# Spreading streamed weights, moving a score step and the mask builds in a one-core two-layer transformer kernel

## The chip, the cores and the metric

The kernel runs on one core of a Trainium2 chip. The metric is the device time of one execution in microseconds (us). The engines in the profile are PE (TensorE, matmuls), PEld (its weight loads), DVE (VectorE), ACT (ScalarE), POOL (GpSimd) and SP (SyncE, which here issues the weight transfers); a "q" behind a name is the engine's sequencer.

## What is computed

Four layers with residuals: A, B, A, B, on 2048 positions of width 640.

```python
x = x + A(layernorm(x), mem0, Wq, Wk, Wv, Wo, seg_len=32)   # 32 heads of 192
x = x + B(layernorm(x), wqkv, wo)                           # 32 heads of 20
# and both once more with the same weights
# A, for each segment s of 32 positions, one after the other:
h = concatenate([mem, xs], axis=1)          # 8 memory rows + 32 positions = 40
q, k, v = h @ Wq, h @ Wk, h @ Wv
p = softmax(where(mask, q @ k.T * scale, -1e9))
o = (p @ v) @ Wo
mem = o[:, :8]                              # the next segment's memory
# B: each position attends to 8 positions at distances 0, 2, ..., 14
```

A is a recurrence over 64 segments. Its four weight matrices together hold 32 units of 960 KB, and not all of them fit in the on-chip memory.

## The kernel before

**Steps.** Both A layers run at once, the second three segments (LAG) behind the first, as two "lanes" of 40 columns, so that one weight load serves 80 columns (NT). There are 67 steps with A work, then two steps with B work only. In step t A works on a segment of each lane, and B, for the two lanes, on what A gave one and two steps ago (b1 and b2).

**Quads.** A step goes over eight quads of four heads. Quad i has projections of V, K and Q (30 matmuls each, L212, tiles ps_v, ps_k, ps_q), transposes of V (a_vt, L240, ps_vt), the output projection of quad i-2 (a_o, L290, ps_acc), the product of probabilities and V of quad i-1 (a_pv, L266 ps_d and L271 ps_o), some B work, and at the quad's end its own scores (a_s, L254 and L255, ps_s). Around the matmuls ACT copies V (VT, L234) and K (KF, Kz, L222 to L224), and DVE copies Q (QT, L229) and transposed V (Vt, L245). Scores go through Exp on ACT (E, L257) and a mask on DVE (E, L258); a_pv needs that E. A softmax denominator goes through Ln and Exp on ACT (R, L274 and L275) and is multiplied in on DVE (OT, L277 to L279); a_o needs that OT. Behind the last quad stand B's K projection (ps_bk), the layer norm of the next step (ln1: ps_st, ln_m, ln_v, ln_r, then hT), a_pv of quad 7, B's V (ps_bv), a_o of quads 6 and 7, and B's Q (ps_bq).

**Weights.** A unit is the 960 KB of one projection of one quad. Sixteen units (N_RES) stay resident, and sixteen are loaded again in every step into a ring of three tiles (w_ring). Resident are all eight output units and the eight Q units (resident_units takes every third of the V, K, Q units in order). V and K of each quad are streamed. A ring transfer is issued on SP (L194), in program order, once the matmuls that used the same ring tile three units earlier are done.

**Order.** All engines run in the order of the code (a manual schedule over PE, ACT, DVE, POOL and SP). Before the first step build_consts builds constants, among them on POOL the masks of layer B (band, L121 to L146), and issues the loads of B's weights from POOL (L173 to L178). prologue then transposes the first inputs, takes segment 0 (x_take, L481, on POOL), and does the first layer norm.

Of the kernel before, what the change touches and what calls it, by code (L numbers as in the profile page):

```python
# [43 lines left out]
def unit_order():  # L44
    order = []
    for i in range(NQUAD):
        order.append(("v", i))
        order.append(("k", i))
        order.append(("q", i))
        if i >= 2:  # L50
            order.append(("o", i - 2))
    order += [("o", 6), ("o", 7)]
    return order


def resident_units():
    res = {("o", i) for i in range(NQUAD)}
    rest = [u for u in unit_order() if u[0] != "o"]
    n = N_RES - NQUAD
    for j, u in enumerate(rest):  # L60
        if (j * n) // len(rest) != ((j + 1) * n) // len(rest):
            res.add(u)
    return res


class Kernel:
    def __init__(self, ctx, tc, A_x, A_mem0, A_Wq, A_Wk, A_Wv, A_Wo, B_wqkv, B_wo, out):
# [17 lines left out]
        self.units = {}  # L85
        self.resident = resident_units()
        self.xr, self.x1, self.ots, self.qxs = {}, {}, {}, {}
        self.x_load(0, self.nc.sync)
        self.m0 = self.xp.tile([P, D], BF16, name="m0", tag="io2")
        self.nc.vector.memset(self.m0[:], 0.0)  # L90
        self.nc.sync.dma_start(out=self.m0[0:NM, :], in_=self.mem0)
        self.build_consts(B_wqkv, B_wo)

    def build_consts(self, B_wqkv, B_wo):
        nc, cp = self.nc, self.cp
# [21 lines left out]
        self.maskA = mA  # L117

        def band(name, cur):
            m = cp.tile([P, NX], BF16, name=name)  # L120
            nc.gpsimd.memset(m[:], 0.0)  # L121
            for half in range(2):
                off = 0 if half == cur else SEG
                for l in range(2):
                    r0 = 64 * half + SEG * l
                    blk = m[r0:r0 + SEG, SEG * l:SEG * (l + 1)]
                    for w in range(BW):
                        nc.gpsimd.affine_select(out=blk, in_=blk, compare_op=ALU.not_equal, fill=1.0,
                                                base=off - BDIL * w, pattern=[[1, SEG]], channel_multiplier=-1)
            return m  # L130
# [18 lines left out]

        def pers(name, shape, n, dt=BF16, zero=True):  # L150
            ts = []
            for j in range(n):
                t_ = cp.tile(shape, dt, name=f"{name}{j}")
                if zero:
                    nc.vector.memset(t_[:], 0.0)
                ts.append(t_)
            return ts

        self.hT = pers("hT", [P, NC * NT + 88], 2)
        self.KF = pers("KF", [P, 4 * NT + 48], 2)  # L160
        self.Kz = pers("Kz", [P, 4 * NT + 48], 2)
        self.VT = pers("VT", [P, 6 * NT + 48], 1)[0]
        self.Vt = pers("Vt", [P, 1152], 2)
        self.xin = pers("xin", [P, NC, NX], 3)
        self.h2T = pers("h2T", [P, NC, P], 1)[0]
        self.KB = pers("KB", [P, NBC, P], 1)[0]
        self.VB = pers("VB", [P, BH // 2, 2 * BD + 1], 1)[0]
        nc.vector.memset(self.VB[:, :, BD:BD + 1], 1.0)
        self.On = pers("On", [P, 3 * P], 1)[0]
        self.YT = pers("YT", [P, NC, P], 1, zero=False)[0]  # L170
        self.m0T = pers("m0T", [P, NC, NM], 1, zero=False)[0]
        self.wqkv = cp.tile([P, NC, 3 * D], BF16, name="wqkv_sb")
# [7 lines left out]
    def unit(self, kind, i):  # L180
        if (kind, i) in self.units:
            return self.units[(kind, i)]
        nc = self.nc
        res = (kind, i) in self.resident
        if kind == "o":
# [40 lines left out]
    def a_q(self, i, t):  # L226
        ps = self.proj_stationary("q", i, t)
        qt = self.ap2.tile([P, 6, NT], BF16, name="QT")
        self.nc.vector.tensor_copy(out=qt[:], in_=ps[:, 0:6 * NT].rearrange("p (a n) -> p a n", a=6))  # L229
        self.qt = qt  # L230

# [15 lines left out]
    def a_s(self, i):  # L247
        nc = self.nc
        ps = self.one("s")
        sv = ps[:, 0:4 * NT].rearrange("p (h n) -> p h n", h=4)  # L250
        kf, kz, qt = self.KF[i % 2], self.Kz[i % 2], self.qt
        for h in range(4):
# [5 lines left out]
        nc.vector.tensor_tensor(out=e[0:NT], in0=e[0:NT], in1=self.maskA[0:NT, :].unsqueeze(1).to_broadcast([NT, 4, NT]), op=ALU.mult)  # L258
        self.em = e

    def a_pv(self, i):
        nc = self.nc
        em = self.em
        vt = self.Vt[i % 2]
# [213 lines left out]

    def x_take(self, t):
        o = SEG * (t % 4)  # L480
        self.nc.gpsimd.tensor_copy(out=self.xin[t % 3][:, :, 0:SEG], in_=self.xt[:, :, o:o + SEG])  # L481

# [18 lines left out]
    def prologue(self):  # L501
# [7 lines left out]
        self.x_transpose(0)  # L509
        self.x_take(0)  # L510
        self.ln1_sq(0)
# [3 lines left out]
    def step(self, t):  # L515
# [5 lines left out]
        for i in range(NQUAD):  # L521
            if a:
                self.a_v(i, t)
                self.a_k(i, t)
                self.a_vt(i)
                self.a_q(i, t)
                if i >= 2:
                    self.a_o(i - 2)
                if i >= 1:
                    self.a_pv(i - 1)  # L530
# [17 lines left out]
            if i == 3 and b1 is not None:  # L548
                self.b_ln_apply(b1)
            if a:  # L550
                self.a_s(i)
            if i == 2:
# [30 lines left out]
    def run(self, ctx):  # L583
        self.x1p = ctx.enter_context(self.tc.tile_pool(name="x1p", bufs=2))
        self.prologue()
        with self.tc.manual_schedule(engines={ENG.PE, ENG.Activation, ENG.DVE, ENG.Pool, ENG.SP}):
            for t in range(self.n_seg + LAG + 2):
# [57 lines left out]
```

## Time and profile before

| | us |
|---|---|
| median of 6 runs | 4010.48 |
| lowest and highest of them | 4002.35 and 4021.05 |
| the profiled execution, whole | 4016.76 |
| its span (first to last instruction) | 4015.1 |
| PE busy | 3438.8 (86%) |
| DVE busy | 2101.4 (52%) |
| ACT busy | 1804.7 (45%) |
| POOL busy | 58.7 (1%) |
| weight queue q1, share of 16 DMA engines | 79.1% |
| mean granted TensorE clock | 0.992 |

Busy time of PE is modelled and overlaps between neighbouring matmuls. What a stretch costs is read from the start times in the timeline: one projection of 30 matmuls starts 1.07 us before whatever follows it at once.

### The profile page before, as it was taken

What the parts mean: (1) busy time and instruction counts of PE and PEld (TensorE: products, weight loads), DVE (VectorE), ACT (ScalarE), POOL (GpSimd) and SP (SyncE); (2) the same over time, 40 slices, a digit from 0 to 9 for tenths busy, and PEclk for the clock granted to TensorE, in tenths of its full rate; (3) what the DMA queues carried; (4) which work ended last, traced back from release to release, by engine and by line L of the source; (5) the groups of instructions that cost most, each with busy time, mean ns of one, the idle gap of its engine ahead of it and who ended that gap; (6) DMA issues with size and microseconds to landing.
All of it is one profiled execution on the core that took longest, in us unless ns stands there. A gap on an engine that the chain in (4) does not pass through costs nothing.

```text
span 4015.1 us, 187722 instructions
## 1 busy us (share of the span) xinstructions
PE 3438.8 (86%) x86260; PEld 3267.3 (81%) x86260; DVE 2101.4 (52%) x6314; ACT 1804.7 (45%) x4924; POOL 58.7 (1%) x186
## 2 busy tenths in 40 slices
PE   4888888888888888888888888888888888888887
PEld 4788888878888888888888888888888888888886
DVE  2455555555555555555555555555555555555554
ACT  2444444444444444444444444444444444444443
POOL 2000000000000000000000000000000000000000
PEclk9999999999999999999999999999999999999998
DMA  9978878877877887787788778878878878887784
GB/s 323 304 262 285 274 264 270 286 261 267 282 265 268 271 278 269 265 287 268 264 280 275 266 256 295 275 263 283 277 263 267 290 269 276 270 292 257 265 280 149
DMA packets 717752, 1090.16 MB, mean 272 GB/s; under 512 B 18008, under 2 KB 715488, under 8 KB 716960
## 3 DMA queue, kind: packets, MB, share of 16 engines
q1 hardware_dynamic: 714912, 1069.79, 79.1%
q8 instruction: 674, 11.04, 1.1%
q0 software_dynamic: 2048, 8.36, 0.6%
q14 instruction: 118, 0.97, 0.1%
HBM read 1075.46 MB, written 2.62 MB: 269 GB/s over the span
## 4 chain that ended last, share of the span: by engine, by line
PE 58%; DMA 22%; issue 9%; DVE 6%; ACT 4%; POOL 0%; SPq 0%; POOLq 0%; ACTq 0%
DMA w_ring<-in_A_Wk_dram 21%; PE ps_k L212 11%; PE ps_acc L290 11%; PE ps_q L212 11%; PE ps_v L212 11%; PE ps_vt L240 3%; PE ps_o L271 2%; ACT R L275 1%; DVE OT L277 1%; PE ps_s L254 1%; PE ps_bq L362 1%; PE ps_d L266 1%; ACT R L274 1%; PE ps_s L255 1%; PE ps_by L453 1%
## 5 line engine op out<-in xcount | busy, mean ns | idle before, releaser
L212 PEld LDWEIGHTS <-w_ring 128*128 128x128 bf16 x32160 | 1207.6, 100 | 346.0 <-DMA w_ring<-in_A_Wk_dram 222.3
L274 ACT ACTIVATE R<-ps_d 128x320 f32<-128x320 f32 x536 | 233.1, 435 | 928.2 <-PE ps_d L266 924.6
L277 DVE TENSOR_TENSOR OT<-ps_o,R 128x320 bf16<-128x320 f32 x536 | 263.5, 492 | 734.4 <-ACT R L275 730.8
L229 DVE CAST QT<-ps_q 128x480 bf16<-128x480 f32 x536 | 352.2, 657 | 300.8 <-PE ps_q L212 300.3
L212 PE MATMUL ps_k<-hT_308,w_ring 128*128 128x80 bf16 x8160 | 347.1, 203 | 135.8 <-DMA w_ring<-in_A_Wk_dram 97.2
L212 PE MATMUL ps_k<-hT_310,w_ring 128*128 128x80 bf16 x7920 | 334.1, 203 | 129.3 <-DMA w_ring<-in_A_Wk_dram 93.9
L234 ACT CAST VT_320<-ps_v 128x480 bf16<-128x480 f32 x536 | 298.2, 556 | 185.4 <-PE ps_v L212 179.8
L245 DVE COPY Vt_322<-ps_vt 80x384 bf16<-80x384 bf16 x536 | 165.7, 349 | 377.9 <-PE ps_vt L240 376.4
L212 PE MATMUL ps_v<-hT_308,w_ring 128*128 128x80 bf16 x8160 | 341.4, 202 | 18.7 <-issue 12.4
L212 PE MATMUL ps_v<-hT_310,w_ring 128*128 128x80 bf16 x7920 | 330.7, 202 | 18.2 <-issue 16.2
L245 DVE COPY Vt_324<-ps_vt 80x384 bf16<-80x384 bf16 x536 | 165.7, 349 | 293.5 <-PE ps_vt L240 291.1
L240 PE MATMUL ps_vt<-ident,VT_320 128*128 128x128 bf16 x3216 | 273.6, 221 | 22.2 <-issue 18.6
L275 ACT ACTIVATE R<-R 128x320 f32<-128x320 f32 x536 | 251.9, 470 | 16.9
L222 ACT CAST KF_314<-ps_k 128x320 bf16<-128x320 f32 x268 | 113.9, 425 | 295.2 <-PE ps_k L212 295.2
L257 ACT ACTIVATE E<-ps_s 80x320 bf16<-80x320 f32 x536 | 229.9, 429 | 29.2 <-PE ps_s L255 25.7
L222 ACT CAST KF_312<-ps_k 128x320 bf16<-128x320 f32 x268 | 113.9, 425 | 285.0 <-PE ps_k L212 285.0
L240 PEld LDWEIGHTS <-VT_320 128*128 128x128 bf16 x3216 | 194.6, 99 | 25.8 <-issue 21.5
L266 PE MATMUL ps_d<-E,ones 80*128 80x320 bf16 x536 | 162.2, 303 | 50.6 <-DVE E L258 49.6
L258 DVE TENSOR_TENSOR E<-E,maskA 80x320 bf16<-80x320 bf16 x536 | 172.1, 321 | 49.7 <-ACT E L257 43.2
L279 DVE TENSOR_TENSOR OT<-ps_o,R 64x160 bf16<-64x160 f32 x536 | 175.5, 327 | 7.4
L271 PEld LDWEIGHTS <-Vt_324 80*128 80x128 bf16 x2144 | 110.4, 98 | 72.6 <-issue 61.7
L278 DVE TENSOR_TENSOR OT<-ps_o,R 64x160 bf16<-64x160 f32 x536 | 163.8, 306 | 0.0
(623 smaller groups left out, 6299.7 us busy)
## 6 DMA issues: line engine op xcount, KB each, us to landing
w_ring<-in_A_Wv_dram SPq DMA_DIRECT2D x536, 960.0 KB, 7.7
w_ring<-in_A_Wk_dram SPq DMA_DIRECT2D x536, 960.0 KB, 6.0
out_dram<-yout POOLq DMA_DIRECT2D x16, 160.0 KB, 5.3
wqkv_sb<-in_B_wqkv_dram POOLq DMA_DIRECT2D x1, 2400.0 KB, 9.1
xr<-in_A_x_dram POOLq DMA_DIRECT2D x15, 160.0 KB, 5.8
w_q_476<-in_A_Wq_dram SPq DMA_DIRECT2D x1, 960.0 KB, 9.7
w_q_602<-in_A_Wq_dram SPq DMA_DIRECT2D x1, 960.0 KB, 8.6
w_q_746<-in_A_Wq_dram SPq DMA_DIRECT2D x1, 960.0 KB
```

Of the source, the lines that this page charges most:

```text
L212: nc.tensor.matmul(ps[:, NT * n:NT * (n + 1)], lhsT=w[:, c, P * n:P * (n + 1)], rhs=hT[:, NT * c:NT * (c + 1)], start=(c == 0), stop=(c == ...
L222: nc.scalar.copy(out=kf, in_=pv[:, :, 0:3:2, :])
L229: self.nc.vector.tensor_copy(out=qt[:], in_=ps[:, 0:6 * NT].rearrange("p (a n) -> p a n", a=6))
L234: self.nc.scalar.copy(out=self.VT[:, 0:6 * NT], in_=ps[:, 0:6 * NT])
L240: nc.tensor.transpose(out=ps[:, n, :], in_=self.VT[:, NT * n:NT * n + P], identity=self.ident[:])
L245: nc.vector.tensor_copy(out=dst, in_=src[:, pr])
L257: nc.scalar.activation(out=e[0:NT], in_=sv[0:NT], func=ACT.Exp, scale=float(DH) ** -0.5)
L266: nc.tensor.matmul(dn[:, 0:4 * NT], lhsT=self.ones[0:NT, :], rhs=em[0:NT, :, :].rearrange("p h n -> p (h n)"), start=True, stop=True)
L274: nc.scalar.activation(out=rf, in_=dn[:, 0:4 * NT], func=ACT.Ln)
L275: nc.scalar.activation(out=rf, in_=rf, func=ACT.Exp, scale=-1.0)
L277: nc.vector.tensor_tensor(out=ot[:, :, 0:3:2, :], in0=ov[:, :, 0:3:2, :], in1=r[:], op=ALU.mult)
L290: nc.tensor.matmul(self.acc[:, NT * c:NT * (c + 1)], lhsT=w[:, m, P * c:P * (c + 1)], rhs=ot[:, m, :], start=(i == 0 and m == 0 and c == 0 ...
```

## The change

Three things change. The tables that say which sixteen units are streamed are replaced: unit_order now gives each unit a position in the step, from costs written by hand, and streamed_units picks for each of sixteen equally spaced positions the nearest unit not yet picked. The result is, in order of use, v0, q0, k1, v2, o0, v3, o1, k4, o2, k5, o3, q6, v7, q7, o5, o6, where the number is the quad. It was v0, k0, v1, k1 and so on to v7, k7. The ring stays at three tiles and sixteen units stay resident.

The scores of quad i are issued behind V of quad i+1 instead of at the end of quad i; those of quad 7 are issued behind the output projection of quad 5 and ahead of a_pv of quad 6. Q copies and E tiles are kept by quad number for that.

The masks of layer B and the loads of B's weights move from build_consts into build_b_consts, called behind the prologue, and the first x_take runs on DVE instead of POOL.

```diff
 def unit_order():
-    order = []
+    order, at = [], 0
+    def use(kind, i, cost):
+        nonlocal at
+        order.append((at, (kind, i)))
+        at += cost
     for i in range(NQUAD):
...
+        use("v", i, 107)
+        use("k", i, 107 + 34)
+        use("q", i, 107)
         if i >= 2:
...
+            use("o", i - 2, 108)
+        at += 70 + 35
+    at += 280
+    use("o", 6, 108)
+    use("o", 7, 108)
+    return order, at + 90
+
+
+def streamed_units():
+    order, total = unit_order()
+    n = N_UNITS - N_RES
+    res = set()
+    for j in range(n):
+        left = [o for o in order if o[1] not in res]
+        res.add(min(left, key=lambda o: abs(o[0] - j * total / n))[1])
     return res
...
-        self.build_consts(B_wqkv, B_wo)
-
-    def build_consts(self, B_wqkv, B_wo):
+        self.build_consts()
+
+    def build_consts(self):
...
+    def build_b_consts(self, B_wqkv, B_wo):
+        nc, cp = self.nc, self.cp
+        def band(name, cur):
...
-        res = (kind, i) in self.resident
+        res = (kind, i) not in self.streamed
...
-        self.qt = qt
+        self.qts[i] = qt
...
-        kf, kz, qt = self.KF[i % 2], self.Kz[i % 2], self.qt
+        kf, kz, qt = self.KF[i % 2], self.Kz[i % 2], self.qts.pop(i)
...
-        self.em = e
+        self.ems[i] = e
...
-        em = self.em
+        em = self.ems.pop(i)
...
-    def x_take(self, t):
+    def x_take(self, t, eng=None):
...
-        self.x_take(0)
+        self.x_take(0, nc.vector)
...
                 self.a_v(i, t)
+                if i >= 1:
+                    self.a_s(i - 1)
                 self.a_k(i, t)
                 self.a_vt(i)
                 self.a_q(i, t)
                 if i >= 2:
                     self.a_o(i - 2)
+                if i == NQUAD - 1:
+                    self.a_s(i)
                 if i >= 1:
                     self.a_pv(i - 1)
...
-            if a:
-                self.a_s(i)
...
         self.prologue()
+        self.build_b_consts(*self.wB)
```

How the instructions move, first on SP, which issues the weight transfers: the first eight ring transfers of step 1. Before:

```order
L194 DMA w_ring_1837<-in_A_Wv_dram 128x5x768
L194 DMA w_ring_1871<-in_A_Wk_dram 128x5x768
L194 DMA w_ring_1980<-in_A_Wv_dram 128x5x768
L194 DMA w_ring_2014<-in_A_Wk_dram 128x5x768
L194 DMA w_ring_2122<-in_A_Wv_dram 128x5x768
L194 DMA w_ring_2156<-in_A_Wk_dram 128x5x768
L194 DMA w_ring_2295<-in_A_Wv_dram 128x5x768
L194 DMA w_ring_2329<-in_A_Wk_dram 128x5x768
```

The same eight places in the changed kernel:

```order
L205 DMA w_ring_1837<-in_A_Wv_dram 128x5x768
L205 DMA w_ring_1914<-in_A_Wq_dram 128x5x768
L205 DMA w_ring_2012<-in_A_Wk_dram 128x5x768
L205 DMA w_ring_2108<-in_A_Wv_dram 128x5x768
L205 DMA w_ring_2230<-in_A_Wo_dram 128x6x640
L205 DMA w_ring_2281<-in_A_Wv_dram 128x5x768
L205 DMA w_ring_2403<-in_A_Wo_dram 128x6x640
L205 DMA w_ring_2501<-in_A_Wk_dram 128x5x768
```

Neighbours in a ring were V and K of one quad, used one right behind the other; now at most one or two units of a quad are streamed, and eight transfers reach to quad 4 instead of quad 3.

Second, ACT at the start of a step in mid-kernel (VT and KF are the copies of V and K, ln_v and ln_r the layer norm of B, E the Exp of the scores). Before:

```order
L234 CAST VT_320<-ps_v 128x480
L222 CAST KF_312<-ps_k 128x320
L223 CAST Kz_316<-ps_k 64x2x80
L224 CAST Kz_316<-ps_k 64x2x80
L326 ACTIVATE ln_v<-ln_v,eps_t 128x64
L328 ACTIVATE ln_r<-ln_v 128x64
L257 ACTIVATE E<-ps_s 80x320
L234 CAST VT_320<-ps_v 128x480
```

In the changed kernel:

```order
L245 CAST VT_114<-ps_v 128x480
L233 CAST KF_106<-ps_k 128x320
L234 CAST Kz_110<-ps_k 64x2x80
L235 CAST Kz_110<-ps_k 64x2x80
L337 ACTIVATE ln_v<-ln_v,eps_t 128x64
L339 ACTIVATE ln_r<-ln_v 128x64
L245 CAST VT_114<-ps_v 128x480
L268 ACTIVATE E<-ps_s 80x320
```

The Exp of quad 0's scores and the copy of quad 1's V have changed places.

Third, ACT behind the last quad (R is the denominator, KB the copy of B's K, VB of B's V). Before:

```order
L274 ACTIVATE R<-ps_d 128x320
L275 ACTIVATE R<-R 128x320
L257 ACTIVATE E<-ps_s 80x320
L368 CAST KB_334<-ps_bk 128x6x64
L326 ACTIVATE ln_v<-ln_v,eps_t 128x64
L328 ACTIVATE ln_r<-ln_v 128x64
```

In the changed kernel:

```order
L268 ACTIVATE E<-ps_s 80x320
L285 ACTIVATE R<-ps_d 128x320
L286 ACTIVATE R<-R 128x320
L379 CAST KB_128<-ps_bk 128x6x64
L337 ACTIVATE ln_v<-ln_v,eps_t 128x64
L339 ACTIVATE ln_r<-ln_v 128x64
```

The Exp of quad 7's scores stands ahead of the denominator of quad 6 instead of behind it; the layer norm and the denominator of quad 7 follow as before.

## Rows read from the trace of the kernel before

**Rows 1.** The page: busy time with instruction counts, and the chain that ended last.

```profile
PE 3438.8 (86%) x86260; PEld 3267.3 (81%) x86260; DVE 2101.4 (52%) x6314; ACT 1804.7 (45%) x4924; POOL 58.7 (1%) x186
PE 58%; DMA 22%; issue 9%; DVE 6%; ACT 4%; POOL 0%; SPq 0%; POOLq 0%; ACTq 0%
```

**Rows 2.** Timeline of PE: V of quad 0 in steps 1 and 66.

```profile
112.26 0.91 PE L212 MATMUL ps_v<-hT_310,w_ring 128*128 128x80 bf16 x21 [0.33 <-DVE hT_310 L304]
3923.62 0.56 PE L212 MATMUL ps_v<-hT_308,w_ring 128*128 128x80 bf16 x11
```

**Rows 3.** Waits of PE from 520 to 3520 us: total, times, longest.

```profile
PE ps_k L212 <- DMA w_ring<-in_A_Wk_dram: 139.9, 155, 2.1
PE ps_k L212 <- issue: 55.3, 38, 2.4
...
PE ps_bt L441 <- issue: 0.2, 1, 0.2
```

**Rows 4.** Timeline of SP and PE, quads 0 and 1, then 6 and 7: start, us, work, idle before.

```profile
2054.70 0.37 SPq L194 DMA_DIRECT2D w_ring<-in_A_Wk_dram  x1
2055.78 0.37 SPq L194 DMA_DIRECT2D w_ring<-in_A_Wv_dram  x1
...
2055.92 1.24 PE L212 MATMUL ps_q<-hT_308,w_q_476 128*128 128x80 bf16 x30
2056.99 0.31 PE L316 MATMUL ps_st<-x_54939,ones 128*128 128x64 bf16 x5
...
2057.91 0.20 PE L254 MATMUL ps_s<-QT,KF_312 128*128 128x80 bf16 x1 [0.46 <-DVE QT L229]
...
2058.18 1.24 PE L212 MATMUL ps_v<-hT_308,w_ring 128*128 128x80 bf16 x30
2060.12 0.35 PE L212 MATMUL ps_k<-hT_308,w_ring 128*128 128x80 bf16 x5 [0.69 <-DMA w_ring<-in_A_Wk_dram]
...
2035.61 1.24 PE L212 MATMUL ps_q<-hT_310,w_q_1452 128*128 128x80 bf16 x30
2039.19 0.99 PE L212 MATMUL ps_v<-hT_310,w_ring 128*128 128x80 bf16 x23
```

**Rows 5.** The page: weight queue and instruction queue: packets, MB, share of 16 engines.

```profile
q1 hardware_dynamic: 714912, 1069.79, 79.1%
q8 instruction: 674, 11.04, 1.1%
```

**Rows 6.** Timeline of PE: two gaps that nothing released, and their neighbours.

```profile
2087.97 0.84 PE L212 MATMUL ps_q<-hT_308,w_q_1275 128*128 128x80 bf16 x19 [1.62 <-issue]
...
2094.47 0.23 PE L212 MATMUL ps_k<-hT_308,w_ring 128*128 128x80 bf16 x2 [1.56 <-issue]
```

**Rows 7.** Stretches of one step: length, busy time by engine, PEclk, DMA share, GB/s.

```profile
2046.20:2058.20 12.00, 10.60 (x269) 9.88 (x266) 7.18 (x22) 5.04 (x14) 0.00 (x0) 1.00 0.43 146
2070.00:2102.00 32.00, 28.41 (x743) 27.54 (x740) 17.23 (x53) 15.41 (x43) 0.00 (x0) 1.00 0.88 286
```

**Rows 8.** Timeline of PE and DVE behind the last quad.

```profile
2048.30 0.30 PE L266 MATMUL ps_d<-E,ones 80*128 80x320 bf16 x1 [0.78 <-DVE E L258]
2051.66 1.06 PE L290 MATMUL ps_acc<-OT,w_o_1800 128*128 128x80 bf16 x25 [0.16 <-DVE OT L279]
...
2047.93 0.32 DVE L258 TENSOR_TENSOR E<-E,maskA 80x320 bf16<-80x320 bf16 x1
2048.28 0.23 DVE L322 TENSOR_SCALAR ln_m<-ps_st 128x64 f32<-128x64 f32 x1
```

**Rows 9.** Start of the kernel: timelines of POOL and SP, then one stretch.

```profile
25.09 0.32 POOL L481 COPY xin_326<-XT_367 128x160 bf16<-128x160 bf16 x1
3.22 1.03 SPq L194 DMA_DIRECT2D w_ring<-in_A_Wv_dram  x1
30.88 0.37 SPq L194 DMA_DIRECT2D w_ring<-in_A_Wk_dram  x1
...
32.00:112.00 80.00, 48.25 (x1107) 43.86 (x1105) 23.02 (x64) 21.59 (x57) 0.00 (x0) 0.98 1.05 367
```

More of the change, by code (lines that the diff above doesn't have):

```diff
@@ L44, in unit_order @@
 def unit_order():
-    order = []
+    order, at = [], 0
[3 more added lines that the diff above has]
+        at += cost
     for i in range(NQUAD):
-        order.append(("v", i))
-        order.append(("k", i))
-        order.append(("q", i))
+        use("v", i, 107)
+        use("k", i, 107 + 34)
+        use("q", i, 107)
         if i >= 2:
[L51 to L62, printed above, removed]
+            use("o", i - 2, 108)
[11 more added lines that the diff above has]
+        res.add(min(left, key=lambda o: abs(o[0] - j * total / n))[1])
     return res
@@ L85, in __init__ @@
         self.units = {}
-        self.resident = resident_units()
-        self.xr, self.x1, self.ots, self.qxs = {}, {}, {}, {}
+        self.streamed = streamed_units()
+        self.wB = (B_wqkv, B_wo)
+        self.xr, self.x1, self.ots, self.qxs, self.ems, self.qts = {}, {}, {}, {}, {}, {}
         self.x_load(0, self.nc.sync)
@@ L117, in build_consts, with pers @@
         self.maskA = mA
+        def pers(name, shape, n, dt=BF16, zero=True):
+            ts = []
+            for j in range(n):
+                t_ = cp.tile(shape, dt, name=f"{name}{j}")
+                if zero:
+                    nc.vector.memset(t_[:], 0.0)
+                ts.append(t_)
+            return ts
+        self.hT = pers("hT", [P, NC * NT + 88], 2)
+        self.KF = pers("KF", [P, 4 * NT + 48], 2)
+        self.Kz = pers("Kz", [P, 4 * NT + 48], 2)
+        self.VT = pers("VT", [P, 6 * NT + 48], 1)[0]
+        self.Vt = pers("Vt", [P, 1152], 2)
+        self.xin = pers("xin", [P, NC, NX], 3)
+        self.h2T = pers("h2T", [P, NC, P], 1)[0]
+        self.KB = pers("KB", [P, NBC, P], 1)[0]
+        self.VB = pers("VB", [P, BH // 2, 2 * BD + 1], 1)[0]
+        nc.vector.memset(self.VB[:, :, BD:BD + 1], 1.0)
+        self.On = pers("On", [P, 3 * P], 1)[0]
+        self.YT = pers("YT", [P, NC, P], 1, zero=False)[0]
+        self.m0T = pers("m0T", [P, NC, NM], 1, zero=False)[0]
+    def build_b_consts(self, B_wqkv, B_wo):
+        nc, cp = self.nc, self.cp
         def band(name, cur):
@@ L148, in build_consts @@
         self.hmask = hm
[L150 to L171, printed above, removed]
         self.wqkv = cp.tile([P, NC, 3 * D], BF16, name="wqkv_sb")
@@ L477, in x_transpose @@
         self.xt = xt
-    def x_take(self, t):
+    def x_take(self, t, eng=None):
         o = SEG * (t % 4)
-        self.nc.gpsimd.tensor_copy(out=self.xin[t % 3][:, :, 0:SEG], in_=self.xt[:, :, o:o + SEG])
+        (eng or self.nc.gpsimd).tensor_copy(out=self.xin[t % 3][:, :, 0:SEG], in_=self.xt[:, :, o:o + SEG])
     def y_store(self, g):
```

## The prediction

> **What bounds the kernel now.** I read the chain of waits first, then the waits of PE, then the timeline of one step. PE is 86% busy and no other engine over 52%, but the chain lies on PE for only 58% of the span; 22% of it is DMA and 9% "issue", time in which PE waited for nothing that the profile shows [rows 1]. So the place to look is what holds PE up. From V of quad 0 in step 1 to the same in step 66 there are 3923.62 - 112.26 = 3811.36 us, or 58.64 us for each of 65 steps [rows 2]. In the 3000 us from 520 to 3520, that is 51.2 steps, PE idled 139.9 us in 155 gaps for a streamed K, and 169.6 us in 175 gaps of "issue" (ten rows of the view, of which the first and the last are shown) [rows 3]. These idle times are counted from modelled ends and come out short: K started 1.94 us after V at 2058.18, where a projection with nothing to wait for hands on after 1.07 us (Q at 2055.92, the next at 2056.99), which makes 0.87 us lost where the row says 0.69 [rows 4]. I add 0.18 us to each gap. A step then loses (139.9 + 155 x 0.18) / 51.2 = 3.3 us to K and (169.6 + 175 x 0.18) / 51.2 = 3.9 us to "issue".
>
> **Why K is late.** K of quad 1 uses the ring tile that V of quad 0 frees. It was issued at 2054.70 and used at 2060.12, 5.4 us later, with PE waiting; the rate was not short, since just before it, from 2046.2 to 2058.2, the DMA engines were 43% busy [rows 4, 7]. The two ring tiles of a quad fall free 1.08 us apart, so transfers come in pairs (2054.70 and 2055.78) [rows 4].
>
> **What "issue" is.** The instruction queue moved 11.04 MB in 674 packets, 16.4 KB each, and PE has 2 x 86260 instructions [rows 1, 5]: 11.04 MB over 172520 is 64 bytes each, so a packet holds 256 PE instructions, 128 matmuls with their loads, and a step (172520 over 67 steps, 2575 instructions) takes 10.06 packets. Two "issue" gaps stand at 2087.97 and 2094.47, 6.50 us apart [rows 6]; between their ends PE ran the last 19 matmuls of Q, then o3, ps_d, ps_o, ps_bt, ps_s, V, and 28 of K, 128 in all. I read the gaps as PE at the end of one packet with the next not there. They follow the weight transfers: from 2070 to 2102, with the DMA engines 88% busy, this step has them; from 2046.2 to 2058.2, at 43%, PE waits for no "issue" at all [rows 7]. In the stretch between, PE stood for K, and the packets caught up. So the fetch competes with the transfers, and a change in when transfers run moves it too. Take away a gap of 1.56 + 0.18 us and a packet's work lasts 4.76 us.
>
> **The change, part by part.**
>
> *Streamed units.* Same number, sixteen of 960 KB. From 32 to 112 us, with the DMA engines never free, they moved 367 GB/s [rows 9]: 983040 bytes take 2.68 us, sixteen 42.9 us, which fits under any step forecast here. A unit is now issued when the one three places earlier is released, 1.07 us after that one's first matmul. The closest such pair in the new order is q6 and o5: q6 started at 2035.61 and v7 at 2039.19, 3.58 us later, with nothing waited for [rows 4]; v7, k7 and q7 add 3.21 us, and transposes and scores a little. Less 1.07 us for q6 itself, at least 5.7 us are left where 5.4 us are needed. All others have six or seven projections from one first matmul to the other, or B's work behind the last quad besides four. So the K waits go: -3.3 us a step. Bounds: all of it, or half, if transfers that queue behind one another still arrive late.
>
> *Instruction fetch.* Now 3.9 us fall on quads 4 to 8, some 32 us or 6.4 packets: 0.61 us a packet. After the change the transfers run through the whole step, so all ten packets meet them, and none is hidden under a wait for K: at 0.61 us each that is 6.1 us, the upper bound. The lower is nothing, as in the 43% stretch. Against the upper bound speaks that pairs are gone: a fetch then found up to two transfers ahead (5.4 us), and now mostly one at some stage of its 2.68 us. With two the packet period was 6.50 us; less 2.68 us, 3.8 us is below the 4.76 us of a packet's work and would not be felt. I take a little under half of the upper bound, 2.9 us, since transfers 3.3 us apart on average with 2.68 us of data each still overlap at times: -1.0 us a step.
>
> The Trainium skill ("Runtime: NRT & Kernel Launch", section "Instruction fetch mechanics") says that instructions come in 16 KiB blocks fetched ahead, and that crossing a block boundary is mostly hidden. The block size agrees with the 16.4 KB a packet above; that it is hidden does not agree with the two gaps. By that rule the gaps would have another cause and stay as they are, which is the third rival.
>
> *Scores behind the next V.* In quad 0 the scores waited 0.46 us for the copy of Q (DVE), 0.64 with the correction [rows 4]. V of quad 1 now covers that: -0.6 us. If V were late, it would be back. The Exp falls behind the copy of V on ACT; K, the transposes and Q (two projections, over 2.1 us) stand between the scores and ps_d, against 0.32 us for the mask [rows 8] and an Exp of similar length, so nothing waits for it.
>
> *Scores of quad 7.* Behind the last quad ps_d waited 0.78 us for E [rows 8]. The scores now run earlier and that wait goes. But nothing is gained: the end is set by a chain on DVE and ACT. OT of quad 6 was followed by the mask of E at 2047.93 and this by ln_m at 2048.28; the layer norm and the denominator of quad 7 on ACT come next, and o7 on PE waited for their OT, to 2051.66 [rows 8]. Without the mask in this chain ln_m could start 0.35 us earlier; but the scores now stand ahead of ps_d of quad 6 (0.28 us of PE), and its denominator waits for one Exp more on ACT (some 0.2 us). The wait moves from ps_d to o7. I count 0; bounds -0.9 and +0.2 us.
>
> *Masks behind the first inputs.* The first x_take stood on POOL behind the masks until 25.41 us [rows 9]. On DVE it can run as soon as the inputs are transposed, at most 16 us earlier. But step 0 must bring in all 32 units and is bound by transfers (share 1.05 from 32 to 112 us) [rows 9]. Four were issued by 3.22 us, enough until about 13 us; the next at 30.88 us, data from 32. Of those 19 idle us the loads of B's weights (3.28 MB, at 367 GB/s 8.9 us) used about nine, and these will now compete. What is won is 19 - 9 = 10 us, once. Bounds 0 and 16.
>
> **Sum.** -3.3 - 1.0 - 0.6 + 0 = -4.9 us a step, 53.7 us instead of 58.64. For the 66 steps from step 1 that is -323 us, and -10 at the start: 4016.8 - 333 = 3684 us against the profiled execution, which lies 6.3 us above the median; so 3677 us.
>
> **Rivals.**
> 1. *Every packet pays.* The fetch term takes its upper bound, 6.1 us: -3.3 + 2.2 - 0.6 = -1.7 us a step, 4010.5 - 112 - 10 = 3888 us. For it: the share of DMA will be near 80% everywhere. Against: the pairs are gone. Chance 0.08. The Trainium skill ("DMA: Bandwidth & Descriptors", section "Queues, rings and completion order") says that each DMA engine takes turns between queues packet by packet; by it a fetch would not stand behind a whole transfer, and undoing the pairs would help less, which leans to this rival.
> 2. *Half of the K waits stay*, as waits for other units: +1.65 us a step, 3677 + 109 = 3786 us. For it: o5 has only some 0.3 to 0.9 us to spare. Chance 0.12.
> 3. *The "issue" gaps have another cause* and stay at 3.9 us: +1.0 us a step, 3677 + 66 = 3743 us. Chance 0.11.
> 4. *Fetch is no longer felt*: -3.9 us instead of -1.0: -7.8 us a step, 4010.5 - 515 - 10 = 3486 us. Chance 0.08.
> 5. *Slower.* Fetch sets the pace: ten packets a step break even with 58.64 us at 5.83 us a packet (58.64 over 10.06). If spread transfers keep a queue at every moment, and packets take 6.0 us on average, against 6.50 us in the pair of gaps read above, a step takes 60.4 us: 4010.5 + 116 - 10 = 4117 us. Against: that needs two transfers ahead all the time, while sixteen of 2.68 us fill 71% of 60.4 us. Chance 0.03.
>
> The forecast itself has 0.58. A fetch term of 1.0 us gives -6.8 us a step and 3550 us; one of 5.2 us gives -2.6 us and 3829 us, which also takes in rivals 2 and 3. I give 3550 to 3830 us; rivals 1, 4 and 5 (0.19) lie outside. A measurement of this kernel can tell about 0.3% (12 us) from no change. Slower by more has the 0.03 of rival 5, within it 0.02 (the far end of rival 1), faster 0.95.
>
> **What would show it.** Right: no wait for w_ring among the larger waits of PE; "issue" near 2.9 us a step and spread over all quads, the quiet start and end of a step included; the wait of ps_s for QT gone; the wait of ps_d for E replaced by one of ps_acc for OT of nearly the same size; step 1 beginning near 102 us. Wrong: waits of ps_acc or ps_q for w_ring; "issue" well over 3.9 us a step; step 1 beginning at 112 us, or before 97.

## The result and the profile after

The changed kernel takes 3691.4 us (median of 10 runs, 3682.18 to 3708.18), against 4015.36 us of the kernel before (20 runs by then). The ratio is 0.9196, 95% interval 0.918 to 0.9211. Forecast were 3677 us and 3550 to 3830 us. The profiled execution took 3697.04 us, its span is 3695.0 us.

The page after: busy time with instruction counts, queues, and the chain that ended last. They answer to [rows 1, 5].

```profile
PE 3380.5 (91%) x86260; PEld 3247.1 (88%) x86260; DVE 2108.2 (57%) x6315; ACT 1791.1 (48%) x4924; POOL 62.5 (2%) x185
q1 hardware_dynamic: 765600, 1069.79, 87.3%
q8 instruction: 674, 11.04, 1.2%
PE 80%; issue 9%; DVE 5%; DMA 4%; ACT 3%; POOL 0%; POOLq 0%; SPq 0%; ACTq 0%
```

The chain that was on PE for 58% is now on it for 80%, and the share of DMA fell from 22% to 4%. "Issue" kept its 9%. The bytes and the instruction packets are the same.

V of quad 0 in steps 1 and 66, the rows that answer to [rows 2]:

```profile
103.07 1.13 PE L223 MATMUL ps_v<-hT_104,w_ring 128*128 128x80 bf16 x27 [0.33 <-DVE hT_104 L315]
3608.48 0.70 PE L223 MATMUL ps_v<-hT_102,w_ring 128*128 128x80 bf16 x15
```

That is 3505.41 us over 65 steps, 53.93 us a step instead of 58.64: 4.71 us less where 4.9 were forecast. Step 1 begins 9.2 us earlier where 10 were forecast.

Waits of PE from 520 to 3520 us (total, times, longest), against [rows 3]:

```profile
PE ps_o L282 <- DVE OT L290: 39.9, 56, 0.9
PE ps_k L223 <- issue: 38.0, 44, 2.2
PE ps_acc L301 <- issue: 26.0, 30, 1.8
PE ps_v L223 <- issue: 24.4, 35, 2.5
PE ps_q L223 <- issue: 21.1, 31, 1.8
PE ps_acc L301 <- DVE OT L290: 12.3, 55, 0.2
...
PE ps_acc L301 <- DMA w_ring<-in_A_Wo_dram: 1.7, 4, 0.5
```

Waits for w_ring are down to 1.7 us in 55.6 steps, from 139.9 us. The gaps of "issue" sum to 146.7 us in 180 gaps (13 rows of the view), which with 0.18 us more for each, as in the prediction, is 3.2 us a step. No row names QT as what the scores wait for. The masked E no longer holds up ps_d; a wait of ps_o for OT of nearly that size stands in its place.

### The profile page after: what moved, and what is told of

Its sections match the earlier page's. It is cut to its first block, busy times and chain, and to the rows that moved or that the text cites. A ratio compares the mean times of both kernels' runs of the same rounds, so it can differ in the third digit from the quotient of the medians.

```text
span 3695.0 us, 187869 instructions
## 1 busy us (share of the span) xinstructions
PE 3380.5 (91%) x86260; PEld 3247.1 (88%) x86260; DVE 2108.2 (57%) x6315; ACT 1791.1 (48%) x4924; POOL 62.5 (2%) x185
## 3 DMA queue, kind: packets, MB, share of 16 engines
q1 hardware_dynamic: 765600, 1069.79, 87.3%
## 4 chain that ended last, share of the span: by engine, by line
PE 80%; issue 9%; DVE 5%; DMA 4%; ACT 3%; POOL 0%; POOLq 0%; SPq 0%; ACTq 0%
PE ps_v L223 15%; PE ps_k L223 15%; PE ps_q L223 15%; PE ps_acc L301 13%; PE ps_vt L251 5%; PE ps_o L282 3%; DMA w_ring<-in_A_Wo_dram 2%; PE ps_s L265 2%; PE ps_s L266 2%; DVE OT L288 2%; PE ps_d L277 2%; PE ps_bk L373 2%; PE ps_bq L373 2%; PE ps_bs L417 1%; PE ps_by L464 1%
## 5 line engine op out<-in xcount | busy, mean ns | idle before, releaser
L223 PEld LDWEIGHTS <-w_ring 128*128 128x128 bf16 x20100 | 776.7, 100 | 88.9 <-issue 67.8
L288 DVE TENSOR_TENSOR OT<-ps_o,R 128x320 bf16<-128x320 f32 x536 | 263.5, 492 | 662.4 <-ACT R L286 610.9
L301 PE MATMUL ps_acc<-OT,w_ring 128*128 128x80 bf16 x12060 | 508.1, 203 | 35.0 <-issue 23.3
L301 PEld LDWEIGHTS <-w_ring 128*128 128x128 bf16 x12060 | 466.5, 100 | 45.3 <-issue 26.5
L223 PE MATMUL ps_v<-hT_102,w_ring 128*128 128x80 bf16 x4080 | 172.0, 202 | 13.3 <-issue 9.0
L290 DVE TENSOR_TENSOR OT<-ps_o,R 64x160 bf16<-64x160 f32 x536 | 175.5, 327 | 7.4
L282 PE MATMUL ps_o<-E,Vt_118 80*128 80x80 bf16 x2144 | 122.8, 201 | 57.1 <-DVE OT L290 48.5
L223 PE MATMUL ps_v<-hT_104,w_ring 128*128 128x80 bf16 x3960 | 165.7, 202 | 7.7 <-issue 6.9
```

What stands on the lines that cost most here:

```text
L223: nc.tensor.matmul(ps[:, NT * n:NT * (n + 1)], lhsT=w[:, c, P * n:P * (n + 1)], rhs=hT[:, NT * c:NT * (c + 1)], start=(c == 0), stop=(c == ...
L282: nc.tensor.matmul(ov[:, pr, b, :], lhsT=vt[0:NT, 512 * pr + w0:512 * pr + w0 + P], rhs=em[0:NT, 2 * pr + j, :], start=st, stop=sp)
L288: nc.vector.tensor_tensor(out=ot[:, :, 0:3:2, :], in0=ov[:, :, 0:3:2, :], in1=r[:], op=ALU.mult)
L301: nc.tensor.matmul(self.acc[:, NT * c:NT * (c + 1)], lhsT=w[:, m, P * c:P * (c + 1)], rhs=ot[:, m, :], start=(i == 0 and m == 0 and c == 0 ...
```

## The experiments

In what follows the fetch term is always the "issue" rows of PE from 520 to 3320 us with 0.18 us added to each gap, per step; by this stretch it is 4.0 us before and 3.2 us after. The ring term is the same for waits for w_ring. A step is the time from V of quad 0 in step 1 to the same in step 66, over 65, from the one profiled execution of each kernel. Ratios are to the kernel before on the same chip; the chips differ between experiments, so kernels are set against one another by their ratios.

| kernel | V of quad 0, step 1 | step 66 | a step | fetch term | ring term |
|---|---|---|---|---|---|
| before | 112.26 | 3923.62 | 58.64 | 4.0 | 3.3 |
| changed | 103.07 | 3608.48 | 53.93 | 3.2 | 0.0 |
| new units alone | 108.21 | 3631.35 | 54.20 | 2.7 | 0.2 |
| scores alone | 113.36 | 3907.85 | 58.38 | 3.6 | 4.0 |
| masks alone | 105.07 | 3935.97 | 58.94 | 4.1 | 3.2 |
| changed, no transfers | 102.83 | 3368.55 | 50.24 | 0 | 0 |
| before, no transfers | 113.77 | 3438.14 | 51.14 | 0 | 0 |
| changed, smaller transfers | 103.61 | 3376.53 | 50.35 | 0.1 | 0 |
| paced halves | 123.88 | 3611.11 | 53.65 | 2.3 | 0.6 |
| unpaced halves | 117.12 | 3620.77 | 53.90 | 3.3 | 0.0 |
| own tile for quad 7 | 102.87 | 3598.94 | 53.79 | 3.2 | 0.1 |
| quad 7 early | 103.78 | 3584.65 | 53.55 | 3.2 | 0.1 |
| paced halves, quad 7 early | 123.94 | 3592.64 | 53.37 | 2.6 | 0.6 |
| layer norm cut in two | 103.01 | 3581.86 | 53.52 | 3.8 | 0.2 |

### The parts alone

Only the new choice of streamed units, in the kernel before:

```diff
-        self.resident = resident_units()
+        self.streamed = streamed_units()
...
-        res = (kind, i) in self.resident
+        res = (kind, i) not in self.streamed
```

> The new choice of streamed units alone; scores and mask builds stay as in the kernel before. Theory (the K waits and part of the issue gaps go, the 0.6 us of quad 0 and the start stay): the measured 4.7 us a step less 0.6 us, times 66, is 270 us off: 3745 us, ratio 0.933, with the wait of ps_s for QT still there. Rival (the fetch of instructions sets the pace, so whatever PE saves elsewhere is given back): the scores' part is worth nothing and this alone gives all but the start, 3700 us, ratio 0.922.

Measured: 3721.65 us, ratio 0.9237 (0.9218 to 0.9256). The rival's 0.922 lies inside the interval, the first reading's 0.933 far outside. A step took 54.20 us, 4.4 us less than before. The wait for QT is there as before:

```profile
PE ps_s L261 <- DVE QT L236: 24.2, 53, 0.5
```

The fetch term was 2.7 us, lower than in the whole change. This part makes most of the gain, and what the other two add on top is less than it would be alone.

Only the scores behind the next V:

```diff
                 self.a_v(i, t)
+                if i >= 1:
+                    self.a_s(i - 1)
...
+                if i == NQUAD - 1:
+                    self.a_s(i)
...
-            if a:
-                self.a_s(i)
```

> The scores behind the next V alone; streamed units and masks as before. Two readings. Sum of parts: 0.6 us a step as predicted for quad 0, 66 times 0.6 is 40 us off: 3975 us, ratio 0.990. Rival, which I hold likelier: with the old units K of quad 1 lands 5.4 us after its issue whatever PE does meanwhile, so the 0.6 us turn into a longer wait of ps_k for w_ring (3.3 to some 3.9 us a step) and the time stays within 10 us of before, ratio 0.998 to 1.001.

Measured: 3994.16 us, ratio 0.9911 (0.9886 to 0.9936). The number is that of the sum of parts, 0.990, and not that of the rival that I held likelier, 0.998 or more. But the rival's mechanism is in the trace, and at its full size: waits of ps_k for w_ring rose from 139.9 to 158.7 us in 3000 us, and V waits for w_ring too.

```profile
PE ps_k L217 <- DMA w_ring<-in_A_Wk_dram: 158.7, 142, 3.1
...
PE ps_v L217 <- DMA w_ring<-in_A_Wv_dram: 16.3, 31, 0.7
```

That is 3.3 before and 4.0 us a step now, so the ring took the 0.6 us of quad 0 back. The time fell all the same, since the fetch term fell from 4.0 to 3.6 us (it is 4.1 in the masks alone, on the same chip), which neither reading had. Why it fell was not tested. That the sum of parts gave the right number here is luck.

Only the masks and the first x_take:

```diff
-        self.x_take(0)
+        self.x_take(0, nc.vector)
...
         self.prologue()
+        self.build_b_consts(*self.wB)
```

> The mask builds behind the first inputs and the first x_take on DVE alone. Theory (step 0 is bound by its 32 units and the loads of layer B's weights): V of quad 0 starts at about 12.4 us as in the changed kernel, but with the old units the ring is full after four transfers instead of six, all the same transfers go on early; step 1 begins 9 to 10 us earlier, ratio 0.9977. Rival (all the 16 us by which PE starts earlier count): ratio 0.996. Rival (B's weights now compete and take it all back): ratio 1.000.

Measured: 4020.41 us, ratio 0.9986 (0.9966 to 1.0005), which by itself can't be told from no change; it rules out the second reading, 0.996, and neither of the others. Its trace is clearer:

```profile
12.38 2.16 PE L216 MATMUL ps_v<-hT,w_ring 128*128 128x80 bf16 x30 [2.48 <-DVE hT L341]
...
105.07 1.09 PE L216 MATMUL ps_v<-hT,w_ring 128*128 128x80 bf16 x26 [0.33 <-DVE hT L308]
```

V of quad 0 started at 12.38 us instead of 28.70, and step 1 at 105.07 instead of 112.26, 7.2 us earlier where 9 to 10 were expected. So 9 of the 16 us were given back in step 0: the first reading's mechanism, with a size that was too large. The new units alone brought step 1 forward by 4.1 us (108.21). There SP issues six weight transfers before it first has to wait for a ring tile, instead of four, which I take to be the reason; together the two make 9.2 us, not 11.

The product of the three ratios is 0.9142, the whole change 0.9196: the parts overlap by some 0.5%, which the widths of the four intervals make uncertain by about 0.4%.

### What "issue" is

The transfers taken away. In the changed kernel and in the kernel before, the ring is three fixed tiles, loaded in step 0 only; from step 1 on the projections use whatever unit lies there, so the results differ and the work is the same.

```diff
-            t_ = self.wring.tile([P, 3840], BF16, name="w_ring")
+            t_ = self.ring[self.nring % RING]
+            self.nring += 1
...
-        nc.sync.dma_start(out=v, in_=src)
+        if res or self.nring <= 16:
+            nc.sync.dma_start(out=v, in_=src)
```

> The changed kernel without its transfers from step 1 on: the three ring tiles keep what step 0 loaded, so projections use wrong weights and only the work is the same. Theory (the issue gaps are PE waiting for its instructions behind weight transfers): with no transfers they are gone, 3.2 us of the 53.96 us of a step; the step takes 50.2 to 50.9 us, the kernel 3465 to 3500 us. Rival (the gaps have another cause, in PE's own issue): they stay at about 3 us a step, and only the few waits for w_ring go: 3680 to 3695 us.

> The kernel before without its transfers from step 1 on (the three ring tiles keep what step 0 loaded; wrong weights, same work). Theory: the K waits (3.3 us a step) and the issue gaps (3.9 us) both go, a step takes 51.0 to 51.6 us, 0.6 us more than the changed kernel without transfers, because the scores of quad 0 still wait for QT: 3510 to 3550 us. Rival (gaps of another cause): only the K waits go, some 55 us a step, 3780 us.

Measured: 3454.42 us, a little under the range expected, and 3524.61 us, inside it; steps of 50.24 and 51.14 us. All waits of PE from 520 to 3320 us, first of the changed kernel without transfers, then of the kernel before without them:

```profile
PE ps_o L286 <- DVE OT L294: 40.0, 56, 0.9
PE ps_acc L305 <- DVE OT L294: 12.6, 56, 0.2
```

```profile
PE ps_d L270 <- DVE E L262: 42.6, 54, 0.8
PE ps_s L258 <- DVE QT L233: 25.2, 55, 0.5
PE ps_acc L294 <- DVE OT L283: 9.0, 55, 0.2
```

There is no "issue" row left in 2800 us. PE runs the same instructions, fetched in 674 packets as before; so the gaps are made by the weight transfers. That they are waits for instructions shows in where they stand. Counted along the whole stretch from 520 to 3320 us, matmuls, weight loads and PE's semaphore instructions together, all 163 gaps of the kernel before stand at the same place in a block of 256 instructions, and so do all 168 of the changed kernel; the prediction had read it from two. The transfers cost the changed kernel 53.93 - 50.24 = 3.69 us a step. The two lists show the scores' move bare: the wait for QT gone, the wait for E turned into one for OT, a step 0.9 us shorter (0.6 were expected).

Then smaller transfers at the same packet size: 3 of 5 or 3 of 6 row blocks of each unit from step 1 on. The other row blocks are left out, so the results differ; PE's work is the same.

```diff
-        nc.sync.dma_start(out=v, in_=src)
+        n = v.shape[1] if res or self.nring <= 16 else 3
+        nc.sync.dma_start(out=v[:, 0:n, :], in_=src[:, 0:n, :])
```

> The changed kernel with smaller transfers from step 1 on: of each streamed unit only three of five (V, K, Q) or three of six (output) row blocks are loaded, 56% of the bytes with packets of the same size; wrong weights, same work. Theory (what counts is how much is queued ahead of a fetch; a packet stalls when more than about 1.9 us of transfers are ahead): with at most 1.6 us in one transfer the gaps nearly go, 0.3 to 0.9 us a step instead of 3.2, 3485 to 3530 us. Rival (what counts is whether a transfer is in flight at all): the gaps shrink with the busy share, to some 1.8 us a step, 3590 us.

Measured: 3467.4 us, 50.35 us a step, better than the theory expected. The stretch from 520 to 3320 us (length, busy by engine, PEclk, DMA share, GB/s), of this kernel and then of the changed kernel:

```profile
520.00:3320.00 2800.00, 2743.68 (x71568) 2664.94 (x71564) 1734.41 (x5221) 1478.79 (x4083) 36.10 (x81) 1.00 0.61 181
```

```profile
520.00:3320.00 2800.00, 2601.58 (x66813) 2504.45 (x66810) 1629.60 (x4881) 1385.20 (x3812) 34.89 (x78) 1.00 0.90 296
```

And its "issue" rows, all of them:

```profile
PE ps_q L227 <- issue: 2.5, 4, 0.9
PE ps_acc L305 <- issue: 1.4, 4, 0.5
PE ps_by L468 <- issue: 0.5, 1, 0.5
```

The DMA engines are busy 61% of the time instead of 90%, two thirds, and the gaps fall to 0.1 us a step, a thirtieth. So the gaps don't follow the busy share in proportion. This run alone can't separate share from depth, since both fell.

Depth can be worked out from the issues and packets in the traces. At the moment PE enters a block of 256 instructions, count the bytes of the weight transfers whose issue has begun, less those that have landed, at 367 GB/s, and see whether PE has a gap at the end of that block. There are 480 blocks before and 522 after, from 520 to 3320 us.

| queued, us | under 0.3 | 0.3 to 1.1 | 1.1 to 1.9 | 1.9 to 2.7 | 2.7 to 3.5 | 3.5 to 4.3 | over 4.3 |
|---|---|---|---|---|---|---|---|
| blocks with a gap, before | 0% | 0% | 0% | 20% | 46% | 55% | 47% |
| blocks with a gap, after | 0% | 0% | 0% | 19% | 56% | 62% | 31% |

Up to 4.3 us the two kernels lie close together. The count is rough at its deep end, because a transfer that was issued a moment ago is in it and need not be ahead of the fetch: with nothing queued, its first packet starts 1.0 us after the issue. On average 2.9 us were queued before and 2.7 us after: the pairs are gone, but the times when nothing was queued are gone too (lowest tenth 0 before, 1.0 us after). What did get rarer is a deep queue, over 3.5 us: 40% of the blocks before, 21% after.

The start of the fetch itself says it more sharply. The instruction packet that belongs to the next block starts 0.2 us (median) after PE enters a block when there are no transfers. Where it started within 2.25 us of that, PE had no gap: 0 of 180 blocks before, 0 of 247 after. Where it started more than 3.5 us later, PE had one in 94 of 119 blocks before and in 54 of 59 after. At a gap, PE went on 2.5 us (median) after the packet's start in both kernels. In the kernel with smaller transfers 1.3 us were queued on average, and no block saw 3.5 us or more.

The Trainium skill ("DMA: Bandwidth & Descriptors", section "Queues, rings and completion order") has a DMA engine take turns between queues packet by packet. By that rule the depth of the weight queue would not matter to a fetch. The two counts above say that it does here.

### Can the queue be kept short at the same bytes?

Each ring transfer from step 1 on issued in two parts; the second part waits on SP for an 8-byte transfer that reads the next copy on ACT or DVE. One kernel with that pacing, one that issues the second part at once.

```diff
+        self.nc.sync.dma_start(out=v[:, 0:3, :], in_=src[:, 0:3, :])
...
+        self.nc.sync.dma_start(out=s[0:1, 0:4], in_=ap)
+        self.nc.sync.dma_start(out=v[:, 3:, :], in_=src[:, 3:, :])
```

> The changed kernel with the same bytes, but each ring transfer of step 1 on in two parts (3 of 5 or 3 of 6 row blocks, then the rest); the second part is held back on SP by an 8-byte transfer that waits for the next copy on ACT or DVE, 1 to 2.5 us later (not for o5, which has no time to spare). Theory (a fetch pays for what is queued ahead of it): the queue ahead falls from mostly 2 to 4 us to mostly under 2, the issue gaps from 3.4 to 1.0 to 2.0 us a step, 3590 to 3640 us, ratio 0.895 to 0.907, at the same share of DMA. Rival (bytes or busy share count, not depth): gaps stay, 3691 us or more, since the later landing brings waits for w_ring.

> As the paced version, but the second part follows the first at once: twice the transfers, no spacing. Theory (depth of the queue): nothing gained, 3685 to 3720 us, ratio 0.918 to 0.926. Rival (smaller single transfers are what helps, by turns between queues): as the paced version, 3590 to 3640 us.

Measured: 3709.75 us, ratio 0.9217 (0.9195 to 0.9239) paced, and 3713.96 us, 0.9229 (0.9206 to 0.9251) unpaced. Neither is better than the changed kernel. The unpaced time is as expected. The paced time is that of the rival, 3691 us or more, and so are its waits for w_ring. Part of the time was lost at the start: in step 0 SP stood in waits with resident units queued behind them, and step 1 began at 123.88 and 117.12 us. In the steps after, the theory holds in its direction but not in its size. The fetch term is 2.3 us paced (1.0 to 2.0 were expected) against 3.3 unpaced, and a step 53.65 against 53.90 us: about half of the saving came back as waits for parts that landed late. These are the rows of the paced kernel from 520 to 3320 us:

```profile
PE ps_k L260 <- DMA w_ring<-in_A_Wk_dram: 12.6, 20, 1.6
...
PE ps_acc L343 <- DMA w_ring<-in_A_Wo_dram: 5.0, 11, 1.2
...
PE ps_v L260 <- DMA w_ring<-in_A_Wv_dram: 4.4, 7, 1.0
```

The pacing also hardly shortened the queue. Counted as in the table above, 2.6 us were queued on average in the paced kernel, and 2.7 us in the unpaced and in the changed one; over 3.5 us were queued at 13% of the blocks instead of 21%. So the queue that the theory spoke of, mostly under 2 us at the same bytes, was not reached, and what it would give stays open. A deeper ring was not tried; a fourth tile could be had by keeping one unit less resident. The unpaced kernel does show that more and smaller transfers at the same queue change nothing.

### The chain behind the last quad

First the suspect that the waits name, the single ps_o tile: quad 7 gets a tile of its own in PSUM, the memory that matmuls write to.

```diff
-        ops = self.one("o")
+        ops = self.one("o") if i < NQUAD - 1 else self.big("ps_o7")
```

> The changed kernel with the product of quad 7 in a PSUM tile of its own (one of the four big tiles) instead of the single ps_o. Theory (behind the last quad a chain on DVE and ACT sets the end: OT of quad 6, layer norm, denominator and OT of quad 7): the wait of ps_o for OT, some 0.9 us a step, moves to ps_acc of quad 7, which waits for its OT; within 0.3% of 3691 us, ratio to before 0.917 to 0.922. Rival (the single ps_o is the cause): 0.8 us a step off, 53 us, ratio 0.906.

Measured: 3689.63 us, ratio 0.9151 (0.9119 to 0.9183); in the trace 53.79 us a step. The wait of ps_o for OT is gone and one of ps_acc for OT L288 has come:

```profile
PE ps_acc L301 <- DVE OT L288: 35.7, 47, 0.8
```

The wait moved, as the chain says; the step is 0.14 us shorter. The ratio is a little under the 0.917 to 0.922 expected. Its interval overlaps that of the changed kernel (0.918 to 0.9211), so a small gain is left open.

Then the chain itself: quad 7's product ahead of the layer norm on all engines.

```diff
-        if nt < T:
-            self.ln1(nt)
-            self.ln1_apply(nt)
         if a:
             self.a_pv(7)
+        if nt < T:
+            self.ln1(nt)
+            self.ln1_apply(nt)
```

> The changed kernel with the product of quad 7 ahead of the next step's layer norm, on all engines, and in a PSUM tile of its own. Theory (behind the last quad the chain OT of quad 6, layer norm, denominator of quad 7, OT of quad 7 sets the end): taking the layer norm out of it frees some 1.0 us a step, 3620 to 3640 us, ratio 0.902 to 0.907. Rival: the layer norm then ends late and V of the next step's quad 0 waits for hT as long: 3685 to 3695 us.

Measured: 3674.32 us, ratio 0.9131 (0.9108 to 0.9153), a step 53.55 us: less than expected, more than nothing. The waits for OT are gone; V of the next step waits for hT instead:

```profile
PE ps_v L223 <- DVE hT L315: 30.3, 48, 0.8
```

With the paced halves on top:

> Paced halves and the early product of quad 7 together. If both theories hold and their gains add, 3520 to 3575 us, ratio 0.877 to 0.891. Rival (a shorter step loads the queue more and the fetch takes back half of it, as between the scores alone and the whole change): 3570 to 3610 us.

Measured: 3687.25 us, 0.9173 (0.9146 to 0.92), slower than both expectations. A step took 53.37 us, and step 1 came late as in the paced kernel (123.94 us). Against the 53.55 us of the early product alone, the pacing again gives only 0.2 us a step.

Last, the layer norm cut in two around OT of quad 7:

```diff
+            m, v = self.ln_moments(ps)
+            xc = self.ln_center(x0, m)
         if a:
             self.a_pv(7)
+        if nt < T:
+            r = self.ln_rstd(v)
+            self.ln_scale(xc, r, self.lanes(self.hT[nt % 2][:, 0:NC * NT])[:, :, :, NM:LT])
```

> The changed kernel with quad 7's product in a PSUM tile of its own, and the next layer norm cut in two: its work on DVE up to the centred input ahead of OT of quad 7, its Ln, Exp and scaling behind. Theory (the chain behind the last quad sets the end; in the early version the whole layer norm on DVE stood between OT of quad 7 and hT, and V waited 0.6 us for hT): both waits go, a step is 52.7 to 53.2 us against 53.55 in the early version, 3625 to 3655 us, ratio 0.903 to 0.910. Rival (the fetch of instructions takes back what the tail gives): a step stays at 53.4 to 53.6 us, 3665 to 3680 us, with more issue gaps.

Measured: 3663.59 us, ratio 0.9105 (0.9081 to 0.913), the best kernel of this study, 1.0% below the changed kernel. A step took 53.52 us in the profiled execution. Its first waits of PE from 520 to 3320 us:

```profile
PE ps_k L223 <- issue: 48.0, 51, 2.4
PE ps_acc L301 <- issue: 36.7, 39, 3.0
PE ps_v L223 <- issue: 28.1, 48, 1.3
PE ps_q L223 <- issue: 26.0, 34, 1.6
```

Waits for OT, E and hT are gone, which with 0.18 us for each gap is 1.3 us a step less than in the changed kernel. But the fetch term rose from 3.2 to 3.8 us with 204 gaps instead of 168, waits for w_ring rose by 0.1 us, and the step fell by only 0.4. The median stands 28 us below that of the changed kernel, the same 0.4 us a step. So the theory was right about the waits and the rival about the step: the chain was broken, and the fetch took about half of it back. Some 0.15 us a step is not accounted for.

## Why the prediction was right, point by point

**K waits, forecast -3.3 us a step.** Right: 0.04 us a step is left. The ring gives each unit the 5.4 us it needs, the closest pair q6 and o5 included; that pair gives three of the four waits there are, on ps_acc.

**Instruction fetch, forecast 2.9 us after, -1.0.** Right in the cause, which the kernels without transfers show, and near in size: 3.2 us, -0.8. The reason given was only half right. I argued that pairs are gone and a fetch finds a shorter queue. Measured, the mean queue was nearly the same (2.9 and 2.7 us), and a block about as likely to end in a gap at a given depth. What fell is mostly the length of a gap: by the "issue" rows from 520 to 3320 us there were 3.4 gaps a step of 0.99 us on average before (163 in 47.7 steps) and 3.2 of 0.82 us after (168 in 51.9). The traces show which got rarer: fetches that started more than 3.5 us late, 119 of 480 blocks before (25%) with 126 of the 161.5 us of gaps behind them, and 59 of 522 after (11%) with 71.5 of 138.1 us. The deep queues did go with the pairs, as the reason says; what it left out is that the empty ones went too.

**Where the gaps stand.** I expected them in all quads and in the quiet end of the step too. They came to the start of the step: 47 of the 168 gaps stand in quads 0 to 2, where before there was none. Behind the last quad there is one, where there were nine.

**Scores of quad 0, forecast -0.6.** Right as a mechanism: the wait is gone, and without transfers the whole scores' move is worth 0.9 us a step. With the transfers it is worth less: on top of the new units a step fell from 54.20 to 53.93 us. The ratios agree: 0.9237 to 0.9196 is 16 us, of which step 1 beginning earlier is 5, and the rest some 0.2 us a step. The fetch term rose meanwhile from 2.7 to 3.2 us. This is the term that was mis-sized, since I added it in full: where fetches come late, more than half of what PE saved elsewhere was lost again. Counted by waits alone, the whole wait for QT went, and the missing 0.2 us a step stand under the fetch.

**Scores of quad 7, forecast 0.** Right, with one detail wrong. Behind the last quad of a step of the changed kernel, PE, then DVE (to set against [rows 8]):

```profile
1927.31 0.30 PE L277 MATMUL ps_d<-E,ones 80*128 80x320 bf16 x1
...
1928.91 0.30 PE L277 MATMUL ps_d<-E,ones 80*128 80x320 bf16 x1
1929.92 0.46 PE L282 MATMUL ps_o<-E,Vt_118 80*128 80x80 bf16 x8 [0.71 <-DVE OT L290]
...
1933.28 1.06 PE L301 MATMUL ps_acc<-OT,w_o_1800 128*128 128x80 bf16 x25 [0.23 <-DVE OT L290]
...
1935.05 1.24 PE L223 MATMUL ps_v<-hT_104,w_ring 128*128 128x80 bf16 x30
...
1929.54 0.33 DVE L290 TENSOR_TENSOR OT<-ps_o,R 64x160 bf16<-64x160 f32 x1
1929.89 0.23 DVE L333 TENSOR_SCALAR ln_m<-ps_st 128x64 f32<-128x64 f32 x1
```

ps_d of quad 7 runs without a wait, and E is not in the chain: ln_m follows OT directly. But ps_o of quad 7 then waits 0.71 us, since the one ps_o tile is still being read by OT of quad 6. I had put that wait at ps_acc. With a tile of its own it does stand at ps_acc, and the time is nearly the same; the chain was right and the first place where PE meets it wrong. From the end of o5 to V of the next step it was 2045.48 to 2053.43, 7.95 us. Now, with the same work in it, it is 1927.03 to 1935.05, 8.02 us.

**Start, forecast -10 us.** Right in size (9.2) and cause: PE starts 16 us earlier and step 0 stays bound by transfers. Of the changed kernel, its first step:

```profile
23.78 1.25 PE L223 MATMUL ps_v<-hT_102,w_ring 128*128 128x80 bf16 x30 [1.11 <-DMA w_ring<-in_A_Wv_dram]
35.27 2.18 PE L223 MATMUL ps_k<-hT_102,w_k_701 128*128 128x80 bf16 x30 [9.96 <-DMA w_k_701<-in_A_Wk_dram]
```

PE gets through two quads and then waits 9.96 us for a resident K, behind the loads of B's weights, as the sum assumed.

**The rivals.** Half of the K waits did not stay. That the gaps have another cause is ruled out by the kernels without transfers. Slower, by a fetch that sets the whole pace, did not come: 5.36 us a packet (53.93 over 10.06), under the 5.83 of its turning point. The first rival, where every packet pays 0.61 us, did not come either: it was 0.32 us a packet (3.2 over 10.06), and 168 of 522 blocks end in a gap. Nor did the fourth, a fetch that is no longer felt.

The Trainium skill ("Runtime: NRT & Kernel Launch", section "Instruction fetch mechanics") calls the crossing of a block boundary mostly hidden. With an empty weight queue the traces agree, with not one gap in 2800 us; with these transfers they don't, with a gap at 163 of 480 crossings before and 168 of 522 after.

## What to carry to other kernels

A wait that the profile puts down to nothing ("issue") deserves a count of the instructions between two of them. Here every gap stood at the same place in a block of 256 PE instructions, which says that PE was out of instructions. What helped against it was less data queued ahead of the fetch; fewer bytes did it (0.1 us a step left), pacing the same bytes did it in part (2.3 us) and lost half of that to late weights. Weights streamed through a small ring should be those whose uses lie evenly apart in time: the ring made a transfer late by its round trip (5.4 us, of which 2.7 us are data), while the DMA engines were 43% busy. Where the fetch sets part of the pace, don't count time saved on the engine elsewhere in full: here 0.9 us a step gave 0.3, and 1.3 us gave 0.4.

## What was not expected of the hardware

The cost of transfers to instruction fetch is steep: at a DMA share of 0.61 with transfers of 0.5 or 0.6 of the size it was 0.1 us a step, at 0.90 with whole ones 3.2 us. And the moved bytes stayed the same while the DMA share went from 0.81 to 0.90 between 520 and 3320 us; the rate went from 273 to 296 GB/s, by 8.4%, in proportion to the shorter step. The share rose by 11%, so most of it is the shorter step and some of it more time for a byte: over the whole page the share times the span is 3176 us before and 3226 us after, 1.6% more for the same bytes, which now go in 765600 packets instead of 714912.
